# Sink copies from GpSimd to VectorE, weight requests between V casts, and earlier crossbar transposes in a fused attention and feed-forward kernel

## The chip, the cores and the metric

One Trainium2 chip, one of its cores. The metric is the device time of one execution in microseconds (us), lower is better. The profiler also gives the span from first to last instruction, which is about 1.7 us shorter than the time. TensorE (PE in the profile, PEld its weight loads), VectorE (DVE), ScalarE (ACT), GpSimd (POOL) and SyncE (SP) run side by side and wait for one another through semaphores.

## The reference, cut to what matters

```python
# batch 4, 8 heads, 768 positions, head size 64; 4 sink positions, window 128
scores = q @ k.T / 8                       # per head
keep   = is_sink | ((rel >= 0) & (rel < 128))
a      = softmax(where(keep, scores, -1e9))
x      = (a @ v) as [3072, 512]
out    = gelu(x @ w_in) @ w_out            # 512 -> 2048 -> 512
```

Each query sees a window of two 128-blocks and four sink positions at the start of the sequence. So the kernel keeps, beside V itself, a small matrix `VST` (in the profile: `vs`) with the sink rows of V, four copies of them, starting at partitions 0, 32, 64 and 96, one for each of the query blocks 2 to 5.

## The kernel before

Heads are worked on in four pairs per batch. Batch 0's attention runs first, by itself (about 5 to 31 us). From then on a batch's up projection runs alone, and its down projection is interleaved, by a list of steps, with the attention of the next batch.

```python
def cast_v(b, p, engine):
    t = STAGE["v", b, p]                                   # fp32, 128 x 768
    copy(engine, V16T[b % 2][p][:, :, :, 0:D], t)          # the V cast, bf16
    for c in range(NBLK - 2):                              # four sink copies, 4 x 128 each
        rows = slice(SKB * c, SKB * c + N_SINK)            # SKB = 32
        copy(engine, VST[b % 2][p][rows, c, :, 0:D], t[0:N_SINK, :, 0, :])

def load_win(g):                                           # 512 of the 2048 columns of w_in
    nc.gpsimd.dma_start(out=WIN[g], in_=...)               # casts fp32 to bf16 on the way

# one pair: values(half) is 12 or 18 small matmuls of TensorE that read et, V16T and VST;
# VectorE then makes rz (reciprocal) and x6 (product); turn() transposes x6 on TensorE and
# VectorE copies the result to XT, which the up projection reads.
    ...
    a[0].values(0)
    a[0].values(1)
    score(a[3], "t0", "sum")
    cast_v(0, 2, nc.gpsimd)
    a[0].turn()
    ...
# first down projection (batch 0), with batch 1's attention mixed in
    (19, lambda: cross(1, 2)),      # VectorE reorders q and k, SP transposes them on the crossbar
    (26, lambda: cross(1, 3)),
    (27, late_values),
    (34, lambda: order(1, 2)),      # VectorE orders what the crossbar delivered
    (40, lambda: order(1, 3)),
```

In the traces of this case VectorE and GpSimd work their instructions in the order in which the program emits them: in run 7 below one line moves, and four sink copies move with it from ahead of VectorE's XT copy to behind it, and in run 9 a weight request that is moved ahead of a V cast starts ahead of it (15.86 and 16.62 us). That order is what most of this change moves. "Crossbar" stands for the transposes that SyncE issues to the DMA (`DMA_TRANSPOSE` in the profile).

The softmax here doesn't subtract the row's maximum and nothing guards it: scores larger than these inputs give would overflow.

## Time and profile before

226.08 us, median of 3 runs (225.56 to 226.23). Three stages, read from TensorE's timeline: "front" ends where TensorE starts to transpose the last K pair of batch 0; "attention 0 and up" ends at the first matmul of the first down projection; "first down" ends at the second up projection.

| stage | from, to (us) | length (us) |
|---|---|---|
| front | 0 to 16.04 | 16.04 |
| attention 0 and up | 16.04 to 47.33 | 31.29 |
| first down | 47.33 to 78.87 | 31.54 |
| rest | 78.87 to 224.38 | 145.51 |

Beside the lines that the prediction shows, one stretch matters: VectorE's timeline in the stage where batch 0's attention ends. Columns: start, duration, engine, line, operation, tiles, shapes, count; in brackets the engine's idle time just before and who ended it.

```profile
16.61 0.96 DVE L117 COPY qkT<-ps_tr 128x768 bf16<-128x768 bf16 x1 [0.50 <-PE ps_tr L231]
17.96 0.20 DVE L343 RECIPROCAL rz<-ps_av 128x6 f32<-128x6 f32 x1 [0.39 <-PE ps_av L335]
18.18 0.56 DVE L344 TENSOR_TENSOR x<-ps_av,rz 128x384 bf16<-128x384 f32 x1
...
20.03 0.56 DVE L366 COPY XT<-ps_tr 128x768 bf16<-128x768 bf16 x1 [0.44 <-PE ps_tr L363]
21.26 0.20 DVE L343 RECIPROCAL rz<-ps_av 128x6 f32<-128x6 f32 x1 [0.67 <-PE ps_av L335]
...
25.70 0.56 DVE L366 COPY XT<-ps_tr 128x768 bf16<-128x768 bf16 x1 [0.44 <-PE ps_tr L363]
```

VectorE is not the bound here.

### The profile page before, as it was taken

What the parts mean: (1) busy time and instruction counts of PE and PEld (TensorE: products, weight loads), DVE (VectorE), ACT (ScalarE), POOL (GpSimd) and SP (SyncE); (2) the same over time, 40 slices, a digit from 0 to 9 for tenths busy, and PEclk for the clock granted to TensorE, in tenths of its full rate; (3) what the DMA queues carried; (4) which work ended last, traced back from release to release, by engine and by line L of the source; (5) the groups of instructions that cost most, each with busy time, mean ns of one, the idle gap of its engine ahead of it and who ended that gap; (6) DMA issues with size and microseconds to landing.
All of it is one profiled execution on the core that took longest, in us unless ns stands there. A gap on an engine that the chain in (4) does not pass through costs nothing.

```text
span 224.4 us, 4615 instructions
## 1 busy us (share of the span) xinstructions
PE 217.8 (97%) x1926; PEld 120.8 (54%) x1926; DVE 92.2 (41%) x182; ACT 118.4 (53%) x141; POOL 71.4 (32%) x134
## 2 busy tenths in 40 slices
PE   7989999999999999999999999999999999999994
PEld 2445756554545555654555555654555565654453
DVE  4456750016997510467857326404657210000010
ACT  4685466586556346669373346669373346651110
POOL 7559982210936667604558600000000000000000
PEclk9999999999999999999999999999999999999999
DMA  6999899999998999987999858200151410001212
GB/s 116 165 216 167 133 184 192 202 196 221 143 227 220 281 328 293 156 146 203 253 244 280 201 123 152 53 3 0 50 125 56 116 47 3 0 0 47 96 47 93
DMA packets 64584, 32.41 MB, mean 144 GB/s; under 512 B 49076, under 2 KB 61620, under 8 KB 64564
## 3 DMA queue, kind: packets, MB, share of 16 engines
q1 hardware_dynamic: 56260, 24.98, 47.6%
q0 software_dynamic: 8304, 7.14, 20.8%
q8 instruction: 15, 0.25, 0.5%
q14 instruction: 5, 0.04, 0.1%
HBM read 27.26 MB, written 6.29 MB: 150 GB/s over the span
## 4 chain that ended last, share of the span: by engine, by line
PE 85%; DMA 4%; ACT 4%; POOL 2%; issue 2%; DVE 2%; POOLq 0%; ACTq 0%; DVEq 0%
PE ps_big L414 36%; PE ps_down L447 34%; PE ps_av L335 6%; DMA c<-in_k_dram 4%; PE ps_big L280 4%; ACT et_t L300 2%; POOL c L103 2%; PE ps_tr L363 1%; ACT gt L426 1%; PE ps_big L294 1%; PE ps_tr L231 1%; DVE qkT L117 1%; PE ps_big L272 1%; PE ps_down L414 0%; DVE x L344 0%
## 5 line engine op out<-in xcount | busy, mean ns | idle before, releaser
L447 PE MATMUL ps_down<-WOUT,gt 128*128 128x512 bf16 (+1 forms) x400 | 91.4, 371 | 0.0
L414 PE MATMUL ps_big<-XT,WIN 128*128 128x384 bf16 x504 | 83.0, 326 | 0.2 <-ACT gt L426 0.2
L426 ACT ACTIVATE gt<-ps_big 128x768 bf16<-128x768 f32 x63 | 50.9, 810 | 42.6 <-PE ps_big L414 42.5
L414 PEld LDWEIGHTS <-WIN 128*128 128x128 bf16 x512 | 49.9, 98 | 33.4 <-issue 0.5
L300 ACT ACTIVATE et_t<-ps_big 128x1024 bf16<-128x1024 f32 x48 | 46.7, 1021 | 24.1 <-PE ps_big L280 22.5
L447 PEld LDWEIGHTS <-gt 128*128 128x128 bf16 x400 | 35.9, 98 | 35.1 <-issue 1.3
L117 DVE COPY osb<-ps_down 128x512 f32<-128x512 f32 (+1 forms) x12 | 8.0, 664 | 46.1 <-PE ps_down L447 46.1
L117 POOL CAST vs<-v_f 4x128 bf16<-4x128 f32 x64 | 23.2, 362 | 2.9
L115 ACT COPY osb<-ps_down 128x512 f32<-128x512 f32 (+1 forms) x13 | 7.4, 572 | 30.0 <-PE ps_down L447 18.7
L335 PEld LDWEIGHTS <-et_t 128*128 128x128 bf16 x480 | 18.4, 97 | 6.3 <-issue 0.2
L117 POOL CAST v<-v_f 128x768 bf16<-128x768 f32 x16 | 14.2, 887 | 20.9 <-DMA v_f<-in_v_dram 19.5
L306 DVE TENSOR_TENSOR et_t<-et_t,maskJ 128x1024 bf16<-128x1024 bf16 (+1 forms) x24 | 17.7, 739 | 7.3 <-ACT et_t L300 7.2
L117 DVE COPY qkT<-ps_tr 128x768 bf16<-128x768 bf16 x10 | 9.4, 955 | 24.6 <-PE ps_tr L231 24.6
L117 POOL CAST c<-qk_f 128x768 bf16<-128x768 f32 x16 | 13.6, 857 | 17.4 <-DMA qk_f<-in_q_dram 12.6
L335 PE MATMUL ps_av<-v,et_t 128*128 128x65 bf16 x352 | 18.9, 193 | 0.0
L344 DVE TENSOR_TENSOR x<-ps_av,rz 128x384 bf16<-128x384 f32 x32 | 17.8, 557 | 1.1
L306 DVE TENSOR_TENSOR et_t<-et_t,mask 128x1024 bf16<-128x1024 bf16 x12 | 9.4, 786 | 17.5 <-ACT et_t L300 17.5
L280 PE MATMUL ps_big<-qkT 64*128 64x256 bf16 x192 | 15.2, 263 | 1.0 <-DVE qkT L117 0.4
L117 DVE COPY qkT<-qP 128x768 bf16<-128x768 bf16 x10 | 8.4, 844 | 18.7 <-DMA qP<-c 18.7
L335 PE MATMUL ps_av<-vs,et_t 128*128 128x65 bf16 x128 | 15.0, 193 | 0.0
L280 PEld LDWEIGHTS <-qkT 64*128 64x128 bf16 x192 | 7.0, 94 | 13.0 <-issue 8.2
L117 DVE COPY qkT<-kP 128x768 bf16<-128x768 bf16 x10 | 8.4, 842 | 3.4 <-DMA kP<-c 3.4
(47 smaller groups left out, 90.4 us busy)
## 6 DMA issues: line engine op xcount, KB each, us to landing
v_f<-in_v_dram SPq DMA_DIRECT2D x16, 384.0 KB, 6.4
out_dram<-osb SPq DMA_DIRECT2D x23, 256.0 KB, 2.3
qk_f<-in_q_dram SPq DMA_DIRECT2D x9, 384.0 KB, 3.7
qk_f<-in_k_dram SPq DMA_DIRECT2D x8, 384.0 KB, 4.4
WIN<-in_moe_w_in_dram POOLq DMA_DIRECT2D x4, 512.0 KB, 5.6
WOUT<-in_moe_w_out_dram POOLq DMA_DIRECT2D x4, 512.0 KB, 12.2
c<-in_k_dram POOLq DMA_DIRECT2D x8, 192.0 KB, 9.6
c<-in_q_dram POOLq DMA_DIRECT2D x7, 192.0 KB, 11.4
```

Of the source, the lines that this page charges most:

```text
L103: nc.gpsimd.dma_start(out=c, in_=rows_of(src, b, p))
L115: engine.copy(out=out, in_=in_)
L117: engine.tensor_copy(out=out, in_=in_)
L231: nc.tensor.transpose(pt[D * hl : D * (hl + 1), i, :], c[:, hl, i, :], ident)
L280: nc.tensor.matmul(ps[:, hl, col : col + nq * P], lhsT=kt[r : r + D, j, :], rhs=qt[r : r + D, j : j + nq, :].rearrange("d i s -> d (i s)") ...
L300: nc.scalar.activation(out=flat, in_=ps, func=AF.Exp, scale=att_scale)
L306: nc.vector.tensor_tensor(out=flat[:, :, 0:col], in0=flat[:, :, 0:col], in1=m.unsqueeze(1).to_broadcast((P, 2, col)), op=ALU.mult,)
L335: nc.tensor.matmul(pv[:, (i - half * n3) * 2 + hl, :], lhsT=lt, rhs=rh, start=(n == 0), stop=(n == len(parts) - 1),)
L344: nc.vector.tensor_tensor(out=self.x6[:, half * n3 : (half + 1) * n3, :, :].rearrange("s i h d -> s (i h) d"), in0=pv[:, :, 0:D], in1=rz.u ...
L414: nc.tensor.matmul(halves[hf], lhsT=WIN[f // 4][:, t, ts(f % 4, P)], rhs=XT[b, t][:, hf * HALF : (hf + 1) * HALF], start=(t == 0), stop=(t ...
L426: nc.scalar.activation(out=to, in_=whole, func=AF.Gelu)
L447: nc.tensor.matmul(po[:, 0:width], lhsT=GT[b, f][:, ts(m, P)], rhs=WOUT[f // 4][:, f % 4, c : c + width], start=(f == 0), stop=(f == NFT - 1),
```

## The change

GpSimd casts V for batch 0, makes the sink copies and asks for all weights. The author wanted to unload it: the sixteen sink copies of batch 0 go to VectorE, so that the weight requests come sooner; the weights then let the q and k loads of batch 1 land sooner, so the crossbar part can be moved forward in the list of steps. One score tile (pair 0's last) is masked by GpSimd selects instead of two mask matmuls.

```diff
-    def cast_v(b, p, engine):
+    def cast_v(b, p, engine, sinks=None):
...
-            copy(engine, VST[b % 2][p][rows, c, :, 0:D], t[0:N_SINK, :, 0, :])
+            copy(sinks or engine, VST[b % 2][p][rows, c, :, 0:D], t[0:N_SINK, :, 0, :])
...
-        score(a[0], "t4", "sum")
+        score(a[0], "t4", "cut")
...
-        cast_v(0, 0, nc.gpsimd)
         score(a[2], "t0", "sum")
         turn_in("q", 3, nc.vector)
-        load_win(0)
         score(a[2], "t2", "sum")
         turn_in("k", 3, nc.vector)
+        cast_v(0, 0, nc.gpsimd, nc.vector)
+        load_win(0)
         score(a[2], "t4", "sum")
-        cast_v(0, 1, nc.gpsimd)
-        load_win(1)
         a[0].values(0)
         a[0].values(1)
+        cast_v(0, 1, nc.gpsimd, nc.vector)
+        load_win(1)
         score(a[3], "t0", "sum")
-        cast_v(0, 2, nc.gpsimd)
+        cast_v(0, 2, nc.gpsimd, nc.vector)
         a[0].turn()
         score(a[3], "t2", "sum")
         a[1].values(0)
         a[1].values(1)
-        cast_v(0, 3, nc.gpsimd)
         load_win(2)
+        cast_v(0, 3, nc.gpsimd, nc.vector)
         load_win(3)
...
-                    (19, lambda: cross(1, 2)),
-                    (26, lambda: cross(1, 3)),
-                    (27, late_values),
-                    (34, lambda: order(1, 2)),
+                    (9, lambda: cross(1, 2)),
+                    (19, lambda: cross(1, 3)),
+                    (20, late_values),
+                    (31, lambda: order(1, 2)),
```

## The prediction

> **What bounds the kernel now.** I read four views in this order: the busy table of the page, the chain that ended last, the timelines of the engines from 14 to 31 us (where the attention of batch 0 runs) and from 50 to 65 us (where the first down projection is mixed with the attention of batch 1), and the stretches of two microseconds.
>
> ```profile
> PE 217.8 (97%) x1926; PEld 120.8 (54%) x1926; DVE 92.2 (41%) x182; ACT 118.4 (53%) x141; POOL 71.4 (32%) x134
> ```
>
> TensorE is busy for 217.8 of 224.4 us. All of its idle time together is 6.6 us, 1.3 us of it before its first matmul, so nothing the change does to another engine can win much: TensorE's own work does not shrink, except for two mask matmuls. The question is only where TensorE waits, and for whom. From the chain:
>
> ```profile
> 6.94 9.05 DMA c<-in_k_dram
> 15.99 0.04 issue
> 16.04 0.53 PE ps_tr L231 x12
> ...
> 24.47 0.21 DVE rz L343
> 24.68 0.02 issue
> 24.70 0.57 DVE x L344
> ...
> 60.58 0.56 DVE et_t L306
> 61.13 1.66 DVE qkT L117 x2
> 62.80 0.05 issue
> 62.84 0.61 PE ps_big L280 x8
> ```
>
> Up to 16.04 us the landing of the last K pair sets the pace; whatever is saved before it is absorbed there. From 16 to 31 us TensorE is the path, with visits to VectorE (24.5 to 25.3). At 62.8 it waits for VectorE's ordering of a crossbar transposed K; its timeline gives 0.39 us of idle time there. The GpSimd timeline shows what the author is after:
>
> ```profile
> 16.34 0.82 POOL L117 CAST v<-v_f 128x768 bf16<-128x768 f32 x1 [0.82 <-DMA v_f<-in_v_dram]
> 17.11 1.32 POOL L117 CAST vs<-v_f 4x128 bf16<-4x128 f32 x4
> 18.38 0.76 POOL L143 DMA_DIRECT2D WIN<-in_moe_w_in_dram  x1
> ...
> 24.94 1.32 POOL L117 CAST vs<-v_f 4x128 bf16<-4x128 f32 x4
> 26.21 1.48 POOL L143 DMA_DIRECT2D WIN<-in_moe_w_in_dram  x2
> ```
>
> Each group of four sink copies takes 1.32 us of GpSimd, in front of the next weight request. TensorE feels the first and third group: the 30 value matmuls of a pair take 0.94 us undisturbed (pair 3, in the chain at 25.66), but 1.31 us for pair 0 (17.45 to 18.76) and 1.31 for pair 2 (23.14 to 24.45), with gaps just before matmuls that read `vs`. So about 0.7 us is there to win. And since the third weight request comes only at 26.21, the DMA runs almost empty:
>
> ```profile
> 26.00:28.00 2.00, 2.00 (x32) 1.48 (x29) 1.57 (x5) 0.00 (x0) 2.00 (x4) 1.00 0.32 30
> ```
>
> Its last two numbers are the DMA's share and GB/s; the neighbouring stretches have 1.21 and 0.93.
>
> **What the Trainium skill says.** Three places bear on the move to VectorE. "VectorE: DVE Perf Modes", section "The perf-mode tier table": a copy between SBUF tiles runs two fp32 elements a cycle, four bf16 ones. The same page, "Two Vector instructions with no wait between them": an instruction whose output starts in another group of 32 partitions than the last one's is held until all earlier ones have finished. "SBUF — State Buffer", section "Who interferes with whom": a VectorE copy in such a two-port mode and a GpSimd instruction exclude one another, "Whoever issues first gets the shared pair for the whole instruction". The trace agrees with the last two:
>
> ```profile
> L481 DVE COPY vs<-vs x7: 221/278/627, 4.0 to 30.7; 128x528 bf16<-128x528 bf16 x7
> L475 DVE MEMSET vs<- x4: 60/60/60, 1.9 to 2.2; 4x2 bf16 x4
> ...
> 29.41 0.63 DVE L481 COPY vs<-vs 128x528 bf16<-128x528 bf16 x1
> ...
> 56.15 1.16 DVE L306 TENSOR_TENSOR et_t<-et_t,mask 128x1024 bf16<-128x1024 bf16 x1 [0.88 <-ACT et_t L300]
> ```
>
> The same copy takes 278 ns, or 627 while GpSimd issues the WOUT requests. The mask product takes 0.69 us, or 1.16 where GpSimd casts V (55.94 to 56.76). And the four memsets of 60 ns each to partitions 0, 32, 64 and 96 fill 0.37 us, one per 0.10 us, while four memsets of 68 ns that all start at partition 0 fill 0.23. No fp32 copy from SBUF runs on VectorE before, so the first statement is not tested yet.
>
> **The change, part by part.**
>
> First, the mask of pair 0's last score tile goes from two matmuls (0.43 us in the chain for such a pair) to GpSimd selects. They stood at 9.3 us, ahead of the waits for the q and k pairs at 14.58 and 16.04. Saved: 0. GpSimd was idle for 1.83 us there, so no harm.
>
> Second, sixteen sink copies go to VectorE. An estimate of one: a 528-element bf16 copy takes 278 ns, of which 132 cycles at the page's 0.96 GHz are 137 ns, so 140 ns are fixed; 128 fp32 elements at two a cycle add 67, together 207 ns. The four copies of a pair write to partitions 0, 32, 64 and 96, so they are held, with the 40 ns that lie between the memsets: 0.25 us each, 1.0 us a pair, 4.0 us in all, against 5.3 us of GpSimd time freed.
>
> Is there room? From the end of the last `qkT` copy (17.57) to the end of the last `x` (27.64) VectorE has 10.07 us. Four pairs of reciprocal and product at 1.4 us and three XT copies at 0.48 are 7.0; 3.0 us are idle. Of these, the 0.44 us before pair 2's XT copy can't be filled, because no sink copies stand there in VectorE's order. After `x` of pair 3 TensorE has 0.25 us of slack (its transposes start at 27.89). So 4.0 us of new work meets 3.0 - 0.44 + 0.25 = 2.8 us of room, and VectorE becomes the path: +1.2 us. The order makes this bite: the sinks of pairs 1 and 2 both stand ahead of XT of pair 0 and of the products of pair 1, for which TensorE's next transposes wait. The 0.7 us of gaps at the value matmuls is won, and lost again at the transposes; it is within this sum.
>
> Third, the ports. The casts of V1 (V1 lands by about 17.9) and V3 (about 21.1) now fall on the sink copies of pairs 0 and 1 or 2, and the weight requests fall on the others. A full collision with a cast costs up to 0.8 us, one with a request 0.35 (627 less 278). Two casts and three requests would be 2.6 us; I expect a third of that, since the copies are short and may slip between: +0.8 us.
>
> Fourth, weights sooner. The first request moves from 18.38 to about 17.1, the third from 26.21 to about 20.5. TensorE never waits for a weight before, except perhaps by little at 24.27, so this saves nothing directly; but the stream of WIN, WOUT and the casting loads of batch 1 moves forward by some 3.5 us (1.2 from the first request, 2.3 from the empty stretch). So the q and k of pairs 2 and 3 are there at step 9 and 19.
>
> Fifth, the crossbar. VectorE now reorders pair 2's q and k at step 31 instead of 34, which is ahead of the mask products of pair 1 (59.80 to 61.13) rather than behind them. The wait of 0.39 us at 62.84 goes. But two 0.84 us copies now stand in front of those products, while only one pair of head copies (0.8 us at 57.79) has left that stretch. From 58.0, in sequence: reciprocal and product 0.75, two ordering copies 1.5 back to back, output copy 0.6, two products 1.2: ready at 62.05 instead of 61.13. TensorE asks for the second of them at about 61.7 and waits 0.3 us. Net -0.1 us.
>
> Sum: 0 + 1.2 + 0.8 + 0 - 0.1 = +1.9 us, so 226.08 becomes 228.0.
>
> **Rivals.** (a) What the author hopes: the copies are cheap, say 0.14 us each and not held, 2.2 us in all; then they fit into the room of 2.8 us, 0.7 us of gaps and 0.4 at 62.84 go, and the time is 225.0 to 225.7. The four `vs` copies of 0.2 us spacing at 4.0 us speak for it, the spaced memsets against it. (b) Full collisions at the ports: VectorE's copies alternate with casts and requests throughout, +3.5 to +5 us, 229.6 to 231. For it: two of four copies at 29.41 were slowed. Against it: GpSimd is idle or out of queue room after about 27 us, and a short copy that is first blocks GpSimd instead. (c) Everything is hidden: VectorE's delay meets TensorE's slack at the transposes, and the wait at 62.84 is merely replaced: 226.1 within 0.3.
>
> **Range and chances.** I give the sum 55 of 100, (a) 22, (b) 10, (c) 13. The range of 225.4 to 230.4 leaves out the ends of (a) and (b). Faster by over 2% would mean 221.6, more than TensorE's idle time allows. Slower by over 2% means 230.6 or more, only the upper half of (b) and a tail of the sum.
>
> **What would show it.** Right, if VectorE is busy without idle time from 17.6 to about 26 us, each sink group takes 1.0 us or more, TensorE's idle time moves from the `vs` matmuls to its x transposes, and the up projection starts 1 to 3 us later than 30.43. Wrong, if a sink group takes 0.6 us or less, if GpSimd's casts are the ones that stretch, or if TensorE still waits at 62.84. Later phases, from 79 us on, should take the same time in both.

## The result, and the profile after

The changed kernel takes 229.41 us (median of 4 runs, 229.06 to 229.78) against 225.93 us for the kernel before in the same rounds: a ratio of 1.0155, 95% interval 1.0128 to 1.0182. A ratio is the mean time of one kernel's runs over that of the other's in the same rounds, so it is not quite the ratio of the two medians. Executions over 1.5% slower than the fastest of the same kernel are left out of the means. The kernel is 3.5 us slower, within the predicted range and 1.4 us above the predicted value; the lower end of rival (b), 229.6 us, is closer.

| stage | before | after | difference |
|---|---|---|---|
| front | 16.04 | 16.72 | +0.68 |
| attention 0 and up | 31.29 | 34.69 | +3.40 |
| first down | 31.54 | 31.09 | -0.45 |
| rest | 145.51 | 145.51 | 0.00 |

The loss is made in some ten microseconds, and 0.45 us is won back. The chain that ended last now runs, for eight microseconds (21.25 to 29.39) without a break, through VectorE (columns: start, duration, what):

```profile
21.25 0.20 DVE vs L117
21.45 0.03 issue
21.49 0.43 DVE vs L117
21.92 0.03 issue
21.95 0.90 DVE vs L117
...
24.51 0.56 DVE XT L366
...
25.90 0.56 DVE x L344
...
28.82 0.57 DVE x L344
29.39 0.04 issue
29.43 0.34 PE ps_tr L363 x3
```

In the kernel before, the same stretch of the chain was TensorE with one visit of 0.8 us to VectorE. Now the sink copies, XT and x follow one another on VectorE, and TensorE comes back into the chain only at 29.43. (Just before 21.25 the chain names the load and the cast of a V, but VectorE was not idle there: its timeline shows no gap from 18.2 to 29.4 us.) What TensorE waits for, in its view of the waits from 8 to 35 us (us in total, times, longest):

```profile
PE ps_tr L363 <- DVE x L344: 2.7, 5, 1.5
...
PE ps_av L335 <- DVE vs L117: 0.4, 1, 0.4
```

The gaps at the matmuls that read `vs` are down to one of 0.4 us; in their place the transposes of x (L363) wait 2.7 us for VectorE's products, a line that the same view of the kernel before does not have. And the copies themselves, by tile (duration in ns: least, median, greatest), first before, on GpSimd, then after, on VectorE:

```profile
L117 POOL CAST vs<-v_f x64: 283/287/814, 17.1 to 127.7; 4x128 bf16<-4x128 f32 x64
```

```profile
L117 DVE CAST vs<-v_f x16: 204/220/895, 18.2 to 27.2; 4x128 bf16<-4x128 f32 x16
```

So VectorE is quicker at an undisturbed copy (204 to 221 ns; the estimate was 207), but seven of its sixteen took 342 to 895 ns. GpSimd's timeline tells where those two longest ones fell:

```profile
17.77 0.77 POOL L143 DMA_DIRECT2D WIN<-in_moe_w_in_dram  x1
18.66 0.83 POOL L117 CAST v<-v_f 128x768 bf16<-128x768 f32 x1
...
21.15 0.75 POOL L143 DMA_DIRECT2D WIN<-in_moe_w_in_dram  x1
21.94 0.83 POOL L117 CAST v<-v_f 128x768 bf16<-128x768 f32 x1
```

The copy of 733 ns starts at 18.83, in the cast that starts at 18.66; the one of 895 ns at 21.95, just behind the cast of 21.94. Each ends 0.08 us after its cast does. The one of 433 ns starts at 21.49, in the request of 21.15. VectorE's timeline gives the groups, pair 0, pairs 1 and 2 together, and pair 3, 5.9 us in all:

```profile
18.17 1.65 DVE L117 CAST vs<-v_f 4x128 bf16<-4x128 f32 x4
...
21.25 3.23 DVE L117 CAST vs<-v_f 4x128 bf16<-4x128 f32 x8
...
26.38 1.02 DVE L117 CAST vs<-v_f 4x128 bf16<-4x128 f32 x4
```

### The profile page after: what moved, and what is told of

It is laid out like the page before. It is cut to its first block, busy times and chain, and to the rows that moved or that the text cites. A ratio compares the mean times of both kernels' runs of the same rounds, so it can differ in the third digit from the quotient of the medians.

```text
span 228.0 us, 4613 instructions
## 1 busy us (share of the span) xinstructions
PE 217.3 (95%) x1924; PEld 120.4 (53%) x1924; DVE 95.5 (42%) x198; ACT 118.5 (52%) x141; POOL 67.1 (29%) x120
## 4 chain that ended last, share of the span: by engine, by line
PE 82%; DMA 5%; DVE 4%; ACT 3%; POOL 3%; issue 2%; SPq 0%; POOLq 0%; DVEq 0%; ACTq 0%
PE ps_big L414 36%; PE ps_down L447 35%; DMA v_f<-in_v_dram 5%; PE ps_av L335 5%; PE ps_big L280 3%; POOL c L103 2%; DVE vs L117 2%; ACT et_t L300 2%; ACT gt L426 1%; DVE x L344 1%; PE ps_big L294 1%; PE ps_tr L231 1%; PE ps_tr L363 1%; DVE XT L366 0%; PE ps_down L414 0%
## 5 line engine op out<-in xcount | busy, mean ns | idle before, releaser
L306 DVE TENSOR_TENSOR et_t<-et_t,maskJ 128x1024 bf16<-128x1024 bf16 (+1 forms) x24 | 17.0, 712 | 7.5 <-ACT et_t L300 7.5
L117 POOL CAST vs<-v_f 4x128 bf16<-4x128 f32 x48 | 18.0, 375 | 2.2
```

Of the source, the lines that this page charges most:

```text
L117: engine.tensor_copy(out=out, in_=in_)
L306: nc.vector.tensor_tensor(out=flat[:, :, 0:col], in0=flat[:, :, 0:col], in1=m.unsqueeze(1).to_broadcast((P, 2, col)), op=ALU.mult,)
```

## The experiments

Eleven more runs were made. In their rounds the kernel before scattered more than in the first measurement (225.58 to 228.61 us), so the ratios have wider intervals, and the stages of the profiles carry more of the argument than differences of a few tenths in the times. All results were correct. The stages of the profiled runs, from TensorE's timeline, in us (run 4 is left out, its profile is of a slow execution):

| run | front | attention 0 and up | first down | ratio to before (95%) |
|---|---|---|---|---|
| before | 16.04 | 31.29 | 31.54 | |
| changed | 16.72 | 34.69 | 31.09 | 1.0155 (1.0128 to 1.0182) |
| changed again | 16.22 | 34.28 | 31.08 | 1.0100 (1.0057 to 1.0143) |
| sinks back on GpSimd | 15.79 | 31.65 | 31.09 | 0.9971 (0.9910 to 1.0033) |
| sinks alone | 15.98 | 36.07 | 31.35 | 1.0174 (1.0112 to 1.0236) |
| sinks on ScalarE | 15.76 | 31.51 | 31.09 | 0.9953 (0.9897 to 1.0010) |
| the same again | 15.99 | 31.38 | 31.09 | 0.9994 (0.9973 to 1.0015) |
| one-port copies | 15.51 | 33.52 | 31.09 | 1.0029 (0.9988 to 1.0070) |
| pair 2's sinks later | 15.78 | 35.89 | 31.08 | 1.0143 (1.0072 to 1.0214) |
| ScalarE and GpSimd | 15.75 | 31.79 | 31.09 | 0.9952 (0.9911 to 0.9993) |
| first weight alone | 16.20 | 30.97 | 31.09 | 1.0021 (0.9983 to 1.0059) |
| crossbar alone | 15.77 | 31.37 | 31.83 | 1.0034 (1.0003 to 1.0066) |

### 1. The sink copies back on GpSimd

```diff
-        cast_v(0, 0, nc.gpsimd, nc.vector)      # and so for pairs 1, 2, 3
+        cast_v(0, 0, nc.gpsimd)
```

> The changed kernel with the sixteen sink copies back on GpSimd; all else as changed. If the copies on VectorE are the whole loss, this is faster than before by the wait of 0.4 us that the earlier crossbar transposes remove: about 225.5 us against 225.9 (ratio 0.998), and the up projection starts near 30.4 us as before. Rival: the 0.7 us by which the transposes of the last K pair start later in the changed kernel (16.72 for 16.04) come from the mask that went to GpSimd; then those 0.7 us stay and this takes 226.2 us or more.

Measured 226.19 us, ratio 0.9971. The loss is gone and the 0.45 us of the first down projection stay won (31.09). The last K transposes started at 15.79, earlier than before (16.04), so the later start in the changed kernel isn't owed to the new mask, which is still in this run. The whole loss is the copies on VectorE. Whether this version is faster than before is left open by its interval.

### 2. The sink copies on VectorE, and nothing else

The kernel before with `cast_v(0, p, nc.gpsimd, nc.vector)` at its old places.

> The kernel before with the sixteen sink copies on VectorE and nothing else. If the copies alone are the loss, up projection starts 3.4 to 4 us later than 30.4 and the wait near 62.8 stays: 229.3 to 230 us. Rival: it is the weight requests between the casts that make the copies slow; before has two of the four requests after the last cast, so the copies would be faster here and the time 228.5 or less.

Measured 230.61 us, ratio 1.0174: the copies alone make a loss of this size. The time is more than I expected, and it does not settle the rival (the weight requests between the casts make the copies slow): here only four of the sixteen copies were stretched (379 to 852 ns) and the groups took 5.2 us instead of 5.9, as the rival has it, while two things that were not in the expectation made the run longer. At the old places the first group stands ahead of the last two `qkT` copies in VectorE's order, so TensorE waited for these too (1.2 us). And the granted clock fell. In the stretches of two microseconds, the third number from the end is the clock:

```profile
18.00:20.00 2.00, 0.80 (x19) 0.46 (x16) 2.00 (x3) 0.49 (x1) 1.83 (x3) 1.00 1.20 211
20.00:22.00 2.00, 0.22 (x4) 0.00 (x0) 1.89 (x7) 1.02 (x1) 1.22 (x2) 1.00 1.19 185
22.00:24.00 2.00, 1.54 (x8) 0.56 (x8) 1.89 (x8) 0.00 (x0) 2.00 (x4) 0.73 1.16 188
24.00:26.00 2.00, 2.00 (x32) 1.57 (x32) 0.90 (x3) 1.02 (x1) 2.00 (x4) 0.50 1.27 194
26.00:28.00 2.00, 2.00 (x46) 1.44 (x44) 1.72 (x7) 0.67 (x1) 1.17 (x2) 0.92 1.18 195
```

TensorE was busy for 0.80 and 0.22 of two microseconds, and then ran at 0.73, 0.50 and 0.92 of its clock: (0.27 + 0.50 + 0.08) x 2 = 1.7 us of clock lost on top of the wait, an estimate. The page "TensorE: Matmul & The Clock Gate", section "Part 1: The HAM clock gate (the "warmup" mystery)", says that an idle window of about 3.4 us brings the half-rate clock; this agrees with the 0.50, except that TensorE was not wholly idle. So of the 4.8 us that this run's second stage is longer than before, an estimate of 3.1 is VectorE's doing. The wait near 62.8, which was to stay, shrank from 0.4 to 0.2 us.

### 3. The sink copies on ScalarE

```diff
-        cast_v(0, 0, nc.gpsimd, nc.vector)      # and so for pairs 1, 2, 3
+        cast_v(0, 0, nc.gpsimd, nc.scalar)
```

> The changed kernel with the sink copies on ScalarE, which has about 5 us idle from 16 to 28 us and whose copies wait for nobody's ports. If VectorE was only a bad home for them: 225.0 to 225.6 us, copies of about 0.3 us each. Rival: taking them from GpSimd is of no use wherever they go, since they delay the exponentials instead: 226 to 227 us.

Measured 225.65 us, ratio 0.9953. Sixteen copies of 281 to 298 ns, none stretched, in the same stage of the program and beside the same casts and requests. Moving the copies away from GpSimd does no harm; moving them to VectorE does. With five rounds on another chip the ratio was 0.9994 (below), so no gain over the kernel before is shown.

### 4. Two V casts taken out of the way (inconclusive)

```diff
-        cast_v(0, 1, nc.gpsimd, nc.vector)      # and so for pair 3
+        cast_v(0, 1, nc.scalar, nc.vector)
```

> The changed kernel with the V casts of pairs 1 and 3 on ScalarE: these are the two that overlap the sink copies of 733 and 895 ns. If VectorE waits there for GpSimd's cast to leave the ports, these two copies fall to about 0.2 to 0.4 us and the time by about 1 us to 228.3 (ratio to before 1.010). If the long copies have another cause (VectorE's own holding, the DMA), they stay long and the time stays at 229.4.

Three of four runs took 235.68 to 236.18 us, the profiled one among them; one took 228.06, as expected. No ratio is given and the 228.06 is a single run. The chain of the profile says what the profiled slow one is:

```profile
15.19 16.08 DMA v_f<-in_v_dram
31.27 0.02 issue
31.29 0.28 DVE vs L117
```

The load of V for pair 3 took 16.1 us instead of 6.2 (14.91 to 21.10 before): without casts in between, GpSimd issued the first two weight requests back to back at 16.70 and 17.46, and VectorE and TensorE stood until 31.3 us. So this run changed the traffic as well as the ports and can't decide about the ports. It needed a cleaner form, which is run 6. That the requests are the cause of the slow load is argued from the order of issue, not shown.

### 5. The changed kernel again

> The changed kernel once more, as the measure for the other runs of this call, and to see which parts of its profile repeat. 229.4 us; four to seven of the sixteen copies between 330 and 900 ns, the others 205 to 221. If the 0.7 us by which the last K transposes started later (16.72 for 16.04) belong to the change, they start near 16.7 again; if they are the chance of how the loads land, anywhere from 15.6 to 16.7.

Measured 229.03 us, ratio 1.0100. The last K transposes started at 16.22 here, and from 15.51 to 16.72 over all profiled runs, whatever the version; the 0.68 us of the front is the chance of how the first loads land, and not part of the change. Six of the sixteen copies took 348 to 734 ns, the others 205 to 221; the two longest, of 731 and 734 ns, again began within a V cast.

### 6. The same copies without the shared ports

```diff
-            copy(sinks or engine, VST[b % 2][p][rows, c, :, 0:D], t[0:N_SINK, :, 0, :])
+            sinks.tensor_reduce(out=VST[b % 2][p][rows, c, :, 0:D],
+                in_=t[0:N_SINK, :, 0, :].unsqueeze(3), op=ALU.max, axis=mybir.AxisListType.X)
```

A maximum over one element is the element. "SBUF — State Buffer", section "Who interferes with whom", says of `tensor_reduce` on trn2 that it never contends with GpSimd, whereas a copy can.

> The changed kernel with the sixteen copies done by VectorE as a maximum over an axis of length one: the same values, one element a cycle, in a form that by the Trainium skill never uses the ports that GpSimd shares. If those ports are what stretches seven copies, all sixteen now take the same 0.27 to 0.3 us, even beside a cast, 5.0 us in all with their gaps instead of 5.9, and the time falls by about 0.9 us to 228.5. If something else holds them, some stay at 0.5 to 0.9 us and, with a slower mode, the time is 230 us or more.

Measured 227.43 us, ratio 1.0029 against 1.0100 for the changed kernel in the same rounds. By tile:

```profile
L143 DVE TENSOR_REDUCE vs<-v_f x16: 265/276/279, 17.0 to 24.7; 4x128 bf16<-4x128 f32 x16
```

And one group beside GpSimd, in VectorE's and then GpSimd's timeline:

```profile
19.57 2.37 DVE L143 TENSOR_REDUCE vs<-v_f 4x128 bf16<-4x128 f32 x8
```

```profile
19.82 0.82 POOL L117 CAST v<-v_f 128x768 bf16<-128x768 f32 x1
20.58 0.75 POOL L149 DMA_DIRECT2D WIN<-in_moe_w_in_dram  x1
```

A whole cast and a whole request lie within the eight copies, and none is longer than 279 ns; the group of pairs 1 and 2 takes 2.37 us where it took 3.23 and 2.86. A slower instruction (276 ns, where an undisturbed copy takes 204 to 221) gives a faster kernel, because it does not queue behind GpSimd. This settles that what stretched the copies is GpSimd's work beside that form of instruction; that the shared ports lie behind it is the page's reason, with which all sixteen agree. All four groups: 1.19 + 2.37 + 1.15 = 4.7 us. The second stage is 0.76 us shorter than in run 5; the front, by chance, another 0.7, so of the 1.6 us between the medians I count about half.

### 7. Pair 2's copies later in VectorE's order

```diff
-        cast_v(0, 2, nc.gpsimd, nc.vector)
         a[0].turn()
         score(a[3], "t2", "sum")
         a[1].values(0)
         a[1].values(1)
+        cast_v(0, 2, nc.gpsimd, nc.vector)
```

> The changed kernel with pair 2's sink copies (and its V cast, the GpSimd order being the same) behind the values of pair 1 in VectorE's order, instead of ahead of pair 0's XT copy. If the loss is that VectorE has too much work, the copies only move and the time stays within 0.5 us of 229.4. If the loss is the order, in which TensorE's transposes of pair 1 wait for copies that they do not need, they come over 1 us sooner and the time is 228.3 or less.

Measured 230.35 us, ratio 1.0143; three of the four runs had a mean clock of 0.993 and the fourth, at 1.000, took 228.61. The waits from 8 to 35 us:

```profile
PE ps_big L414 <- DVE XT L366: 1.4, 1, 1.4
PE ps_tr L363 <- DVE x L344: 1.1, 4, 0.4
```

The transposes wait only 1.1 us instead of 2.7, and a new wait of 1.4 us stands at the up projection, for XT. The work was moved and the wait moved with it. The profiled run then lost clock as run 2 did (0.68, 0.50 and 0.96 from 28 to 34 us, an estimate of 1.7 us). The one run at full clock, 228.61, lies between the two expectations, 0.2 us below the lowest of the changed kernel's in these rounds. The profile decides for too much work, rather than its order: the groups took 5.5 us here, 2.7 more than the room of 2.8 that the prediction found, and the second stage, less the 1.7 us of clock, is 2.9 us longer than before.

### 8. Half on ScalarE, half on GpSimd

Sinks of pairs 0 and 2 on ScalarE, of pairs 1 and 3 on GpSimd, else as changed.

> The changed kernel with the sink copies of pairs 0 and 2 (the ones TensorE waited for before) on ScalarE and those of pairs 1 and 3 on GpSimd. With all sixteen on ScalarE, TensorE still lost 0.6 us to a late exponential of pair 3 and a late copy. If that comes from ScalarE being full, this is faster than that run by about 0.5 us: 225.0 us, ratio to before about 0.993. Rival: it changes nothing beyond 0.1 us since the landing of the last K pair and TensorE's own work set the time: 225.5.

Measured 225.81 us, ratio 0.9952 (0.9911 to 0.9993). The gain that I had expected over run 3 did not come. TensorE's timeline shows what took its place:

```profile
24.74 0.50 PE L414 MATMUL ps_big<-XT,WIN 128*128 128x384 bf16 x2 [1.14 <-DMA WIN<-in_moe_w_in_dram]
```

The first weight was asked for at 16.89, 1.5 us earlier than before (18.38), and landed later (24.69 for 23.99). I take it that the second request (19.82) and the V loads shared the DMA with it; that is argued from the times, not shown.

### 9. The first weight by itself, ScalarE again, and the crossbar alone

First the run that was to remove that wait: `load_win(0)` ahead of the first V cast, `load_win(1)` after the third, else as run 8.

> As the run before it (sink copies of pairs 0 and 2 on ScalarE, 1 and 3 on GpSimd), but the first weight is asked for ahead of the first V cast and the second only after the third cast. In that run TensorE waited 1.1 us at 24.7 us for the first weight, whose load had taken 7.8 us since the second, third and a V load shared the DMA with it. If that wait is the last that can be taken away here, the first weight lands before 23 us, the up projection's long run starts at 29.6 to 29.9 us and the time is 224.6 to 225.2 us, ratio to before about 0.992. If V or K loads are slowed by it instead, TensorE waits there and the time stays at 225.8.

The weight was asked for at 15.86, 1.03 us sooner than in run 8, and landed at 22.90, 1.8 us sooner; the wait is gone, and the second stage is the shortest of all (30.97). But the six runs spread from 225.57 to 228.03, the ratio is 1.0021, and the expected 224.6 to 225.2 us did not come. The profiled run's span was 223.8; why other runs of it are 2 us longer was not profiled and stays open.

> All sixteen sink copies on ScalarE once more, with five rounds, to compare on one chip: 225.6 us, ratio to before 0.995 to 0.998.

226.30 us, ratio 0.9994: within 0.3% of before. No version that I ran is shown to beat the kernel before by a margin that repeats.

The last one takes the kernel before and changes only the four step numbers of the crossbar part.

> The kernel before with only the four steps of the crossbar part changed. Its q and k of pairs 2 and 3 landed at about 52 to 55.6 us, so VectorE now waits for them at the new place. If the later landing still suffices, the wait of 0.4 us near 62.8 goes as it did in the changed kernel, and the down projection with its mixed-in attention takes 31.1 us instead of 31.5: ratio 0.998. If the crossbar part needs the weights to be asked for sooner, VectorE is held at the first mask products and TensorE waits at the first values or scores: 31.5 us or more, ratio 1.000 to 1.004.

Measured 226.76 us, ratio 1.0034, and the first down projection took 31.83 us instead of 31.54. VectorE's timeline:

```profile
53.10 0.36 DVE L158 COPY c<-c 128x768 bf16<-128x768 bf16 x1 [0.58 <-DMA c<-in_k_dram]
...
55.91 0.36 DVE L158 COPY c<-c 128x768 bf16<-128x768 bf16 x1 [0.98 <-DMA c<-in_k_dram]
```

At the earlier step VectorE waits for the K loads of pairs 2 and 3, 0.58 and 0.98 us, and the mask products behind them come too late for TensorE. With the weights asked for sooner (all versions above with 31.09) those loads are there. So the two parts belong together: the steps alone cost 0.3 us, both save 0.45. The sooner requests with the old steps ran only in run 2, along with the sink copies on VectorE: there the stage took 31.35 us, 0.2 less than before.

## Why the prediction was right or wrong, point by point

The range and the direction held; the cause named was the right one. Two terms of the sum were mis-sized, and they err in opposite directions. Without the front, the stages of the changed kernel make +3.40 - 0.45 = 2.95 us, where the sum has 1.9: 0.9 instead of 1.2 for work without room, 2.2 instead of 0.8 for the ports, -0.45 instead of -0.1 for the crossbar, and 0.3 that no term has. The other 0.7 us of the profiled difference are the front's, by chance.

- **TensorE is the bound, and only its waits can change.** Right: the rest of the program takes 145.51 us in both. But the 6.6 us of idle time that the prediction gives do not by themselves rule out a gain of 4.5 us (221.6): 1.3 us of them lie before TensorE's first matmul and 3.2 after its last (221.21 to 224.38), so that 2.2 remain, and with these the statement holds.
- **The mask to GpSimd saves and costs nothing.** Right by run 1, where the front is as short as before with the new mask in place. The front of the profiled changed kernel was 0.68 us longer; run 5 and the others show a spread of 1.2 us there, by chance.
- **A copy of 0.25 us, four microseconds in all.** Right: 204 to 221 ns, and gaps of 31 ns in the groups of pairs 0 and 1, 13 to 14 ns in much of the others. Undisturbed, the sixteen would have taken 3.7 us. Two of the readings that led there were loose, without effect: at 4.0 us stand three `vs` copies, not four, and the mask product that was shown for the ports is a product of two tensors, not a copy, so that it does not bear on the sentence quoted.
- **2.8 us of room, so VectorE becomes the path.** Right: groups of 5.9 us less the room of 2.8 make 3.1 us, and the second stage grew by 3.40; for run 5, 5.5 less 2.8 against 2.99; for the one-port form, 4.7 less 2.8 = 1.9 against 2.23. The sum is 0.3 us short each time.
- **The ports: "I expect a third of that".** Here the prediction failed in size. It expected 0.8 us; the copies took 5.9 instead of 3.7 us, so 2.2: two casts cost 1.2 and five requests 1.0, against two and three for 2.6 in the stated whole. The reason given for a third of it ("may slip between") held only for single copies: seven of the twelve that began within a request kept their 204 to 221 ns. But VectorE worked without a pause, so in five of the eight requests beside its copies one copy was caught, and in both casts that stood in its way the copy that started within the cast lasted until the cast's end.
- **Weights sooner save nothing directly.** Right where it was tested, and in run 8 the first weight, asked for sooner, landed later, and TensorE waited 1.1 us for it.
- **The crossbar, "Net -0.1 us".** Mis-sized: it is -0.45 us. The step that failed is that TensorE would wait 0.3 us for the second mask product of pair 1. TensorE's timeline has the wait of 0.39 us before, and after the change neither that one nor one for the product (first line before, then after):

```profile
62.84 0.61 PE L280 MATMUL ps_big<-qkT 64*128 64x256 bf16 x8 [0.39 <-DVE qkT L117]
```

```profile
65.58 0.41 PE L335 MATMUL ps_av<-v,et_t 128*128 128x65 bf16 x8
65.83 0.19 PE L335 MATMUL ps_av<-vs,et_t 128*128 128x65 bf16 x1
...
66.48 0.61 PE L280 MATMUL ps_big<-qkT 64*128 64x256 bf16 x8
```

The last line is the same matmul group as the first. The second product ends at 66.02, as worked out (61.93 without the 4.09 us by which this stage starts later; 62.05 was predicted). But it multiplies columns 0 to 383 only, and the sink scores that the matmul at 65.83 reads are in the last 128 columns of that tile, which come straight from the exponential. I had read the tile's name and not the columns.

- **Rivals.** The hope (a), cheap copies that fit the room, falls: even undisturbed a copy takes 0.22 us, not 0.14, and the sixteen 3.7 us, more than the room of 2.8. Of (b), the ports throughout, the mechanism is true, and its lower end of 3.5 us lies close to the second stage's 3.40: the outcome lies between the sum and this rival, to which the prediction gave 10 of 100. (c), all hidden, falls.
- **The signs named.** VectorE had no idle time of more than a few hundredths from 18.2 to 29.4 us; TensorE's waits went from the `vs` matmuls to the x transposes; the long run of the up projection started at 34.52 for 30.43; GpSimd's casts did not stretch (0.82 to 0.83 us). All as said, the start somewhat later than "1 to 3 us".

## What to carry to other kernels

Before moving work to an engine because it is quicker at it or less busy, add up the gaps that it has in that very stage, leave out those that its instruction order cannot fill, and see whether the work fits; a share of 41% over the whole program says nothing of a stage in which it is needed seven microseconds out of ten. If the new home is VectorE and the old one GpSimd, look at what GpSimd does at the same time: the copies of this change waited for its casts and DMA requests, and a slower instruction that did not, or ScalarE, was the better choice. When one part of a change makes data come sooner and another uses it sooner, test both and each: here the second alone was a loss of 0.3 us, and both together a gain of 0.45.

## What the Trainium skill lacked or had wrong

- "SBUF — State Buffer", "Who interferes with whom": that a VectorE copy waits for a GpSimd instruction is there; of GpSimd's issuing of a DMA the page tells only the reverse, that VectorE can hold it up, and it does not say which part of a request blocks VectorE. In the changed kernel the five copies that began 0.29 to 0.48 us before the end of such a request (each some 0.75 us long) lasted until just after its end (342 to 523 ns); the seven that began elsewhere in one took 204 to 221.
- The same section says that `tensor_reduce` never contends on trn2. Confirmed: sixteen took 265 to 279 ns beside casts and requests. It does not mention that it can serve as a copy.
- "VectorE: DVE Perf Modes", "The TRN2 errata — SBUF-src ops pay a fixed extra latency per instruction": the table's row for VectorE, (58 + 128/2) cycles at 0.96 GHz, gives 127 ns for the sink copy, where 204 to 221 ns were measured. The page says itself that the row gives too little and that about 150 cycles were measured for the fixed part; an estimate with these, (150 + 64) / 0.96 = 223 ns, comes close.
- "VectorE: DVE Perf Modes", "Two Vector instructions with no wait between them": it says which instructions are held, without the cost. Here held copies started 13 to 31 ns after the end of the one before; why 13 in some groups and 31 in others is open.
- "TensorE: Matmul & The Clock Gate", "Part 1: The HAM clock gate (the "warmup" mystery)": it names an idle window of some 3.4 us, but not how little work counts as idle. In run 2 no single wait was longer than 1.9 us and TensorE was busy for 1.02 of 4 us, and the clock still fell to 0.50; in run 7 it fell after 1.93 of 4 us (24 to 28); in the changed kernel, at 0.46 busy of one 2 us stretch (24 to 26), it stayed at 1.00.
